# Column halves for the last output bank, and a third scratch pair for the first weight narrowings

## Chip, cores and metric

The kernel runs on one core of one Trainium2 chip. The metric is the device time of one execution in microseconds (us), as the median of several runs.

## What is computed

A Nyström attention, then a gated two-layer network, then a second two-layer network, all in float32 precision. Cut to what matters:

```python
# q, k, v: (4 batches, 8 heads, 576 tokens, 64); 32 landmarks are means of 18 tokens each
A  = softmax(q @ k_lm^T / 8);  Bm = softmax(q_lm @ k_lm^T / 8);  C = softmax(q_lm @ k^T / 8)
Z  = Bm^T / (norms);  six times: Z = 2 Z - Z @ Bm @ Z
x  = (A @ Z @ C @ v)                      # as 2304 tokens x 512
xn = x / rms(x) * rms_g
x  = (silu(xn @ w_gate) * (xn @ w_val)) @ w_out          # 512 -> 1536 -> 512
out = (s * relu(x @ w_in2)**2 + b) @ w_out2              # 512 -> 2048 -> 512
```

The five weight matrices arrive as float64 words and are narrowed to float32 on the chip.

## The kernel before, in words

**One list, planned ahead.** The kernel does not emit instructions as it goes. It first makes a list of operations (`op`), each with the engines that may run it, an estimated duration, a key (its due time) and the buffers that it reads and writes. Then `Scheduler.run` (line 174) walks through estimated time, and at each step gives an engine the ready operation with the smallest key. What it emits is a fixed order for each engine's queue and for SP's DMA queue; on the chip each engine runs its queue in that order and waits where data is not there. A `Ring` is a set of slots; a `Buf` takes a free slot of its ring when its first operation is emitted, and gives it back after its last. A queued ring hands out slots in the order in which its Bufs were made. `gate` (line 1485) is an operation of no cost that waits for a list of others and then frees slots that were marked as held.

**The first network's start.** Weights are handled in 12 column blocks `f` of 128. `first_weights` (line 1167) narrows block f of w_gate and of w_val into one of three slots of `rawg`, and stores the result to DRAM for later batches (`keptg`). `narrow` (line 1112) does one matrix block: SP loads 512 KB of float64 words into a staging slot; ScalarE (ACT) writes two scratch tiles, `ca_all` (line 1145) and `cmag_all` (lines 1147 and 1155; in place of 1155 VectorE, DVE, can run 1156); DVE combines the two into the destination (line 1159). The scratch tiles have two slots each (`ca_r`, `cm_r`, line 358), so two narrowings can be between their first ACT instruction and their DVE combination at a time. `fused` (line 1289) multiplies the narrowed block by the batch's value matrix on TensorE (PE) into two PSUM banks (line 1299), and ACT and DVE evacuate it as `u` (lines 1311, 1312, 1314). `hidden` (line 1337) then runs the products of u with the normalised attention rows (line 1326) and the gated activation (ACT line 1343, DVE lines 1345 and 1349). `fused` and `hidden` share four banks, `gv_r`, two of which batch 1's attention also uses. `out_weights` (line 1181) narrows blocks of w_out into two slots of `rawo` (`ro_r`, line 355); these are first written when block 0 of w_out is combined.

**The end.** The second network's output is accumulated token block by token block (`second_mm`, line 1407): 128 tokens by 512 columns fill one PSUM bank, three products (high and low parts) for each of 16 blocks f. The last token block, `j = NB - 1`, has 256 tokens, two banks (`c` = 0 and 1). After its last block f, each bank is copied to a staging tile by one ACT or DVE instruction (lines 1426 and 1427) and stored by four transfers of 32 rows, two from SP's queue and two from ACT's (line 1432). A transfer's 32 rows lie 18 output rows apart; the four groups of 32 are neighbours: row 18 i + n for i = 0 to 31, and n rises by one from one transfer to the next.

Of the kernel before, what the change touches and what calls it, by code (L numbers as in the profile page):

```python
# [38 lines left out]
N_SUM = 2  # L39
XB = 1  # L40
# [233 lines left out]
def t_dma(kb, n=1):  # L274
    return DMA_LAG + max(DMA_KB * kb, 0.45 * n)
# [10 lines left out]
def t_mm(n):  # L286
    return 0.0004167 * (max(n, 200) + 32)
# [7 lines left out]
def tile_nystrom_attention_two_mlps(  # L295
# [62 lines left out]
    ca_r, cm_r = (Ring([Slot(x[:, 512 * i:512 * i + 512]) for i in range(2)], True) for x in c_all)  # L358
# [753 lines left out]
    def narrow(key, kind, f, part, dst, w, after=()):  # L1112
# [3 lines left out]
        st, a, m = Buf(st0_r if rows else st_r), Buf(ca_r), Buf(cm_r)  # L1116
# [45 lines left out]
        if rows:  # L1162
            row_ops.extend(S_.ops[n_ops:])
        for o in S_.ops[n_ops + 1:]:
            o.after = RELC
# [240 lines left out]

    def second_mm(key, j, f, w, wn, hs, off):
# [5 lines left out]
        for c in range(nt):  # L1413
            def mm(_, c=c):
                s = slice(off + 128 * c, off + 128 * c + 128)
                for i, (a, y) in enumerate(PART3):
                    nc.tensor.matmul(out=A[c].t, lhsT=hs[a].t[:, s], rhs=w.t[:, 512 * y:512 * y + 512],  # L1417
                                     start=(f == 0 and i == 0), stop=(f == F2 - 1 and i == 2))

            op(("pe", 3 * t_mm(512)), key + 0.65 * c, mm, r=[*wn, *hs], w=[A[c]]).mode = "r"  # L1420
        if f < F2 - 1:
            return
        for c in range(nt):
# [12 lines left out]
            if j < NB - 1:  # L1436
                op(("sp", t_dma(256, 4)), key, lambda e, store=store: store(e, range(4)), r=[o])
                continue
            op(("sp", t_dma(128, 2)), key, lambda e, store=store: store(e, (0, 1)), r=[o])
            op(("act", 1.1), key, lambda e, store=store: store(e, (2, 3)), r=[o])  # L1440
# [83 lines left out]

    n_out = [0]
# [7 lines left out]
    for n in range(N_T):  # L1533
        t = T[n]
        todo = len(o_at.get(n, []))
        if n < len(units):
            b, f = units[n]
            if n == F1:
                gate("near", row_ops, t)
            if f == 0:  # L1540
                if b + 1 < B:
                    attention(b + 1, *at_time(b + 1))
                    S_.by_path(batch_ops[b + 1], *at_time(b + 1))
                else:
                    gate("attn", at_ops, t, free_w2)
            u = us.pop((b, f))
            hidden(t, t + 0.85, b, f, 0, u)
            t += 2 * t_first
# [234 lines left out]
```

## Time and profile before

| | |
|---|---|
| median of 3 runs | 829.31 us (828.41 to 831.85) |
| profiled execution, its own time | 829.26 us |
| its span (first to last instruction) | 827.5 us |
| PE busy | 810.5 us, 98% |
| weight loads of PE | 653.3 us, 79% |
| DVE busy | 651.0 us, 79% |
| ACT busy | 531.4 us, 64% |
| GpSimd (POOL) busy | 119.8 us, 14% |

How to read it: the busy shares are averages over stages with different limits. PE's busy time holds 43 matmuls on a constant that only keep it active before the first products, and matmuls that wait inside a group. So a stage has to be read by itself: which engine is full there, and what the first useful work waits for.

### The profile page before, as it was taken

To read this page: it belongs to the slowest core of one execution; us is meant where nothing else is said; L and a number is where in the kernel's file an instruction comes from. 1 tells how busy PE (TensorE), PEld (TensorE's weight loads), DVE (VectorE), ACT (ScalarE), POOL (GpSimd) and SP (SyncE) were. 2 spreads that over 40 slices of the span, in tenths; PEclk is the share of its full clock that TensorE was granted. 3 is DMA by queue.
4 is the path that set the end of the run, shared out by engine and by line. 5 is a ranking of instruction groups with operands and counts; after the bars stand their busy time and mean duration, and the time that the engine had idled before them with its cause. 6 is when DMAs were issued, how large, how long until landed. Compare 5 with 4: busy or idle time off the path is not lost.

```text
span 827.5 us, 16641 instructions
## 1 busy us (share of the span) xinstructions
PE 810.5 (98%) x6151; PEld 653.3 (79%) x6151; DVE 651.0 (79%) x1461; ACT 531.4 (64%) x1097; POOL 119.8 (14%) x173
## 2 busy tenths in 40 slices
PE   8899999999999999999999999999999999999997
PEld 5577767877787877888888888887888888888886
DVE  6888998777787777898998988799766767665554
ACT  5899987543534434688888976578555556565553
POOL 0370355117411132210100000000000000000000
PEclk9999999999999999999999999999999999999999
DMA  9999959652542313398978641232422432254234
GB/s 281 326 381 368 266 178 285 222 135 81 144 139 89 128 47 125 116 295 274 321 260 316 199 169 51 90 102 70 135 77 76 112 93 80 75 164 140 64 87 130
DMA packets 87234, 138.46 MB, mean 167 GB/s; under 512 B 26480, under 2 KB 49008, under 8 KB 87152
## 3 DMA queue, kind: packets, MB, share of 16 engines
q1 hardware_dynamic: 86960, 137.13, 52.3%
q8 instruction: 48, 0.79, 0.4%
q14 instruction: 34, 0.28, 0.1%
q10 hardware_dynamic: 192, 0.26, 0.1%
HBM read 114.82 MB, written 22.54 MB: 166 GB/s over the span
## 4 chain that ended last, share of the span: by engine, by line
PE 79%; DVE 11%; ACT 5%; DMA 2%; issue 2%; POOL 0%; DVEq 0%; SPq 0%; ACTq 0%; POOLq 0%
PE bank L1417 23%; PE bank L1282 17%; PE bank L1390 14%; PE bank L1326 14%; PE bank L1664 3%; PE bank L1299 3%; PE bank L754 1%; DVE w_all L1108 1%; DVE hl L1108 1%; DVE hbuf L1345 1%; PE bank L1372 1%; ACT ca_all L1145 1%; PE bank L675 1%; DMA stage<-in_moe_w_out_dram 1%; DVE rawg L1159 1%
## 5 line engine op out<-in xcount | busy, mean ns | idle before, releaser
L1417 PE MATMUL bank<-w_all,hh 128*128 128x512 f32 x472 | 148.0, 394 | 0.0
L1390 PE MATMUL bank<-hh,w_all 128*128 128x512 f32 (+1 forms) x448 | 144.6, 379 | 0.1
L1417 PEld LDWEIGHTS bank<-w_all,hh 128*128 128x128 f32 x472 | 88.2, 188 | 20.3
L1390 PEld LDWEIGHTS bank<-hh,w_all 128*128 128x128 f32 x448 | 81.6, 188 | 24.1 <-issue 9.5
L1417 PE MATMUL bank<-w_all,hl 128*128 128x512 f32 x236 | 93.1, 394 | 0.0
L1326 PE MATMUL bank<-xh,u_all 128*128 128x288 f32 x400 | 88.2, 300 | 0.5 <-DVE hbuf L1345 0.3
L1390 PE MATMUL bank<-hl,w_all 128*128 128x512 f32 (+1 forms) x224 | 83.0, 370 | 0.0
L1108 DVE TENSOR_TENSOR w_all<-rawo,w_all 128x512 fp32r<-128x512 f32 x86 | 62.1, 722 | 12.8 <-ACT w_all L1106 10.0
L1326 PEld LDWEIGHTS bank<-xh,u_all 128*128 128x128 f32 x400 | 66.2, 188 | 4.6 <-issue 1.0
L1343 ACT ACTIVATE hbuf<-bank 128x288 f32<-128x288 f32 x96 | 38.9, 405 | 32.4 <-PE bank L1326 30.2
L1326 PE MATMUL bank<-xl,u_all 128*128 128x288 f32 x200 | 59.0, 295 | 0.2 <-DVE xl L1090 0.2
L1326 PE MATMUL bank<-xh,xl 128*128 128x288 f32 x184 | 54.2, 295 | 0.0
L1326 PE MATMUL bank<-xl,xh 128*128 128x288 f32 x184 | 54.2, 294 | 0.0
L1417 PEld LDWEIGHTS bank<-w_all,hl 128*128 128x128 f32 x236 | 44.3, 188 | 10.6
L1345 DVE SCALAR_TENSOR_TENSOR hbuf<-hbuf,bank 128x288 f32<-128x288 f32 x96 | 42.5, 443 | 8.8 <-ACT hbuf L1343 8.3
L1106 ACT ACTIVATE w_all<-rawo 128x512 fp32r<-128x512 f32 x48 | 30.3, 631 | 28.7 <-PE bank L1390 14.6
L1390 PEld LDWEIGHTS bank<-hl,w_all 128*128 128x128 f32 x224 | 42.2, 188 | 5.5 <-DVE hl L1108 0.3
L1106 ACT ACTIVATE hh<-hbuf 128x288 fp32r<-128x288 f32 (+8 forms) x73 | 26.6, 389 | 21.9 <-PE bank L1390 13.9
L1585 ACT ACTIVATE xbuf<-xbuf,b_sb,s_sb 128x512 f32<-128x512 f32 (+1 forms) x34 | 26.0, 765 | 20.2 <-DVE xbuf L1596 19.7
L1155 ACT ACTIVATE cmag_all<-stage 128x512 f16<-128x512 f32 x48 | 37.9, 790 | 1.0
L1326 PEld LDWEIGHTS bank<-xl,u_all 128*128 128x128 f32 x200 | 37.6, 188 | 1.2 <-DVE xl L1090 0.4
L1108 DVE TENSOR_TENSOR hl<-hbuf,hh 128x512 fp32r<-128x512 f32 (+8 forms) x76 | 36.9, 495 | 1.6 <-ACT hh L1106 0.2
(316 smaller groups left out, 1940.3 us busy)
## 6 DMA issues: line engine op xcount, KB each, us to landing
rawg<-keptg SPq DMA_DIRECT2D x36, 512.0 KB, 4.4
stage<-in_moe_w_out_dram SPq DMA_DIRECT2D x28, 512.0 KB, 5.5
rawo<-kepto SPq DMA_DIRECT2D x48, 256.0 KB, 3.1
rawg<-kept SPq DMA_DIRECT2D x24, 512.0 KB, 3.6
rawo<-kept SPq DMA_DIRECT2D x36, 256.0 KB, 2.6
stage<-in_moe_w_in_dram SPq DMA_DIRECT2D x16, 512.0 KB, 5.4
keptg<-rawg SPq DMA_DIRECT2D x12, 512.0 KB, 6.1
kept<-tail SPq DMA_DIRECT2D x24, 256.0 KB, 3.7
```

Source lines behind the costliest of these rows:

```text
L1106: e.activation(out=hi(), in_=src(), func=ACTF.Copy) if e is nc.scalar
L1108: b = op({"dve": t_dve(n), "pool": t_pool(n)}, key, lambda e: e.tensor_tensor(out=lo(), in0=src(), in1=hi().bitcast(F32), op=ALU.subtract) ...
L1155: e.activation(out=upper(), in_=word(1).bitcast(F32), func=ACTF.Copy, scale=2.0 ** -100)
L1282: nc.tensor.matmul(out=ps.t, lhsT=a[h][:, 128 * kd:128 * kd + 128], rhs=x[kd][y].t, start=(first and kd == 0 and i == 0), stop=(last and k ...
L1299: nc.tensor.matmul(out=pU[g].t[m, 256 * j:256 * j + 256], lhsT=gw[b].t[p, m], rhs=r.t[p, :, 128 * k:128 * k + 128], start=True, stop=True)
L1326: nc.tensor.matmul(out=ps.t[:, 0:HC], lhsT=u[a].t[:, 256 * g + 128 * part:256 * g + 128 * part + 128], rhs=x[y].t.rearrange("p k n -> p (k ...
L1343: op(("act", t_act(HC)), tg, lambda e: e.activation(out=th.t[:, 0:HC], in_=pg.t[:, 0:HC], func=ACTF.Tanh, scale=0.5), r=[pg], w=[th])
L1345: op(("dve", t_dve(HC)), tg, lambda e: e.scalar_tensor_tensor(out=th.t[:, 0:HC], in0=th.t[:, 0:HC], scalar=1.0, in1=pg.t[:, 0:HC], op0=ALU ...
L1390: nc.tensor.matmul(out=A[c].t[:, 0:n], lhsT=w[a].t[:, 128 * c:128 * c + 128], rhs=hs[y].t[:, 0:n], start=(f == 0 and i == 0), stop=(f == F ...
L1417: nc.tensor.matmul(out=A[c].t, lhsT=hs[a].t[:, s], rhs=w.t[:, 512 * y:512 * y + 512], start=(f == 0 and i == 0), stop=(f == F2 - 1 and i = ...
L1585: e.activation(out=h.t[:, c:c + n], in_=h.t[:, c:c + n], func=ACTF.Identity, scale=s_sb, bias=b_sb) if e is nc.scalar
L1664: nc.tensor.matmul(out=ps.t[:, 0:n], lhsT=tot.t[:, 1024 * a + c:1024 * a + c + 128], rhs=xs[3, kd // 2][y].t[:, n * (kd % 2):n * (kd % 2) ...
```

## The change

There are two edits, which do not touch each other.

**The last bank.** In the last block f of the last token block, the products of the last bank (c = 1) are issued for columns 0 to 255 and then for columns 256 to 511: six matmuls of 256 columns in place of three of 512. A new function, `last_out`, copies both banks of the last token block in two halves of 256 columns: for each half ACT or DVE, but for the last half of the last bank DVE alone. Bank c = 0 is stored by one transfer from SP of 128 rows by 512 columns; bank c = 1 by one transfer from ACT for the first half and one from SP for the second, each of 128 rows by 256 columns. The transfer's destination is indexed (n, i, column) with n = 0 to 3 and i = 0 to 31; its source is 128 partitions by columns.

**The third scratch slot.** The narrowings of w_gate and w_val for f = 0, 1, 2 (`C_F = 3`, six narrowings) take their scratch from rings with a third slot: `rawo`'s slot 0 as `ca`, `rawo`'s slot 1 as `cmag`. Both slots of `rawo` are held until a gate has seen all six through, and then serve w_out as before. The six have queues of their own (`ca0_r`, `cm0_r`) on the shared slots.

```diff
+C_F = 3
-    ca_r, cm_r = (Ring([Slot(x[:, 512 * i:512 * i + 512]) for i in range(2)], True) for x in c_all)
+    c_two = [[Slot(x[:, 512 * i:512 * i + 512]) for i in range(2)] for x in c_all]
+    ca_r, cm_r = (Ring(x, True) for x in c_two)
+    c_more = [Slot(ro_r.slots[0].t), Slot(ro_r.slots[1].t.bitcast(I32))]
+    ca0_r, cm0_r = (Ring(x + [y], True) for x, y in zip(c_two, c_more))
+    c_ops = []
+    for x in ro_r.slots:
+        x.held = True
...
-        st, a, m = Buf(st0_r if rows else st_r), Buf(ca_r), Buf(cm_r)
+        early = rows and f < C_F
+        st, a, m = Buf(st0_r if rows else st_r), Buf(ca0_r if early else ca_r), Buf(cm0_r if early else cm_r)
...
+        if early:
+            c_ops.extend(S_.ops[n_ops + 1:])
...
+    def last_out(key, j, A):
+        c0, n = blocks[j]
+        nt = n // 128
+        for c in range(nt):
+            o = Buf(os_r)
+            for d in range(2):
...
+                e = {"act": t_act(256), "dve": t_dve(256)} if c < nt - 1 or d == 0 else {"dve": t_dve(256)}
+                op(e, key, copy_out, r=[A[c] if c < nt - 1 else (A[c], d), "stage"], w=[(o, d)])
+
+            def store(e, x, m, ds, c=c, o=o):
+                bb, n_ = divmod((c0 + 128 * c) // 32 + x, SEG)
+                cols = slice(256 * ds[0], 256 * ds[-1] + 256)
+                e.dma_start(
+                    out=out[bb * S:bb * S + S, :].rearrange("(i n) d -> n i d", n=SEG)[n_:n_ + m, :, cols],
+                    in_=o.t[32 * x:32 * x + 32 * m, cols])
+
+            if c < nt - 1:
+                op(("sp", t_dma(256, 1)), key, lambda e, store=store: store(e, 0, 4, (0, 1)), r=[(o, 0), (o, 1)])
+                continue
+            op(("act", 0.5), key, lambda e, store=store: store(e, 0, 4, (0,)), r=[(o, 0)])
+            op(("sp", t_dma(128, 1)), key, lambda e, store=store: store(e, 0, 4, (1,)), r=[(o, 1)])
...
+            halves = 2 if j == NB - 1 and f == F2 - 1 and c == nt - 1 else 1
+            for d in range(halves):
+                def mm(_, c=c, d=d, m=512 // halves):
...
+                        nc.tensor.matmul(out=A[c].t[:, m * d:m * d + m], lhsT=hs[a].t[:, s],
+                                         rhs=w.t[:, 512 * y + m * d:512 * y + m * d + m],
...
+        if j == NB - 1:
+            last_out(key, j, A)
...
-            op(("sp", t_dma(128, 2)), key, lambda e, store=store: store(e, (0, 1)), r=[o])
-            op(("act", 1.1), key, lambda e, store=store: store(e, (2, 3)), r=[o])
...
+    def free_c(_):
+        for x in ro_r.slots:
+            x.held, x.free = False, 0.0
...
+            if n == 2:
+                gate("c", c_ops, -1.0, free_c)
```

## Rows read from the trace of the kernel before

**Rows 1.** Windows: stretch, length, busy of PE, PEld, DVE, ACT, POOL (instructions), clock, DMA

```profile
0.00:39.20 39.20, 34.12 (x472) 20.22 (x473) 30.34 (x113) 26.66 (x66) 6.29 (x14) 1.00 1.03 309
39.20:49.70 10.50, 8.38 (x77) 5.87 (x75) 9.24 (x18) 10.27 (x21) 9.20 (x12) 1.00 1.04 335
49.70:80.00 30.30, 30.30 (x299) 25.04 (x294) 26.40 (x68) 29.30 (x59) 6.28 (x10) 1.00 1.04 376
80.00:120.00 40.00, 37.84 (x475) 27.89 (x476) 37.45 (x92) 35.34 (x79) 16.28 (x22) 1.00 0.86 251
823.40:827.50 4.10, 0.00 (x0) 0.00 (x0) 0.63 (x1) 0.00 (x0) 0.00 (x0) 0.90 0.46 128
```

**Rows 2.** Timeline of PE, 37 to 50 us: start, duration, engine, line, operation

```profile
37.91 1.68 PE L1746 MATMUL bank<-ones 128*128 128x512 bf16 x7
39.24 0.48 PE L1326 MATMUL bank<-xh,u_all 128*128 128x288 f32 x1
...
39.69 0.42 PE L1326 MATMUL bank<-xh,u_all 128*128 128x288 f32 x2
39.95 0.30 PE L1326 MATMUL bank<-xl,u_all 128*128 128x288 f32 x1
...
46.33 1.22 PE L1299 MATMUL bank<-rawg,gw 64*32 64x256 f32 x16 [0.88 <-DVE hbuf L1345]
...
48.75 0.99 PE L1299 MATMUL bank<-rawg,gw 64*32 64x256 f32 x16 [0.40 <-DVE u_all L1314]
49.67 0.40 PE L1326 MATMUL bank<-xh,u_all 128*128 128x288 f32 x1
```

**Rows 3.** Timeline of ACT, 26 to 35 us

```profile
26.07 0.67 ACT L1145 ACTIVATE ca_all<-stage 128x512 f32<-128x512 f32 x1
...
27.32 0.78 ACT L1155 ACTIVATE cmag_all<-stage 128x512 f16<-128x512 f32 x1
30.64 2.53 ACT L1043 ACTIVATE region<-bank 128x288 f32<-128x288 f32 x8 [2.54 <-PE bank L1037]
...
33.25 0.75 ACT L1145 ACTIVATE ca_all<-stage 128x512 f32<-128x512 f32 x1
```

**Rows 4.** Timeline of DVE, 30 to 46 us

```profile
31.99 0.76 DVE L1048 TENSOR_TENSOR region<-region 128x576 f32<-128x576 f32 x1 [0.85 <-ACT region L1043]
...
36.24 0.66 DVE L1159 SCALAR_TENSOR_TENSOR rawg<-ca_all,cmag_all 128x512 int32<-128x512 int32 x1
...
40.36 0.68 DVE L1159 SCALAR_TENSOR_TENSOR rawg<-ca_all,cmag_all 128x512 int32<-128x512 int32 x1
...
43.15 2.76 DVE L1159 SCALAR_TENSOR_TENSOR rawg<-ca_all,cmag_all 128x512 int32<-128x512 int32 x2
```

**Rows 5.** Timeline of all engines, the last 6 us; SPq and ACTq are DMA issues

```profile
822.46 0.62 PE L1417 MATMUL bank<-region,hh 128*128 128x512 f32 x2
822.65 0.60 ACT L1426 ACTIVATE stage<-bank 128x512 f32<-128x512 f32 x1 [4.31 <-PE bank L1417]
...
822.91 0.39 PE L1417 MATMUL bank<-region,hl 128*128 128x512 f32 x1
823.28 1.75 SPq L1432 DMA_DIRECT2D out_dram<-stage  x4
823.28 1.83 ACTq L1432 DMA_DIRECT2D out_dram<-stage  x4
823.33 0.69 DVE L1427 COPY stage<-bank 128x512 f32<-128x512 f32 x1 [3.12 <-PE bank L1417]
```

**Rows 6.** DMA, 823 to 827 us: queue, packets, MB, share of 16 engines

```profile
q1 hardware_dynamic: 192, 0.26, 29.7%
q10 hardware_dynamic: 192, 0.26, 17.7%
```

**Rows 7.** DMA, 46.8 to 48.6 us, when rows of 1 KB were loaded

```profile
q1 hardware_dynamic: 655, 0.65, 109.7%
```

**Rows 8.** DVE timeline: a copy of 256 columns out of a PSUM bank

```profile
47.82 0.42 DVE L1312 CAST u_all<-bank 128x256 fp32r<-128x256 f32 x1
```

More of the change, by code (lines that the diff above doesn't have):

```diff
@@ L1405, in tile_nystrom_attention_two_mlps, with copy_out @@
     acc = {}
+    def last_out(key, j, A):
[4 more added lines that the diff above has]
+            for d in range(2):
+                def copy_out(e, c=c, d=d, o=o):
+                    x, y = o.t[:, 256 * d:256 * d + 256], A[c].t[:, 256 * d:256 * d + 256]
+                    if e is nc.scalar:
+                        e.activation(out=x, in_=y, func=ACTF.Copy)
+                    else:
+                        e.tensor_copy(out=x, in_=y)
+                e = {"act": t_act(256), "dve": t_dve(256)} if c < nt - 1 or d == 0 else {"dve": t_dve(256)}
[11 more added lines that the diff above has]
+            op(("sp", t_dma(128, 1)), key, lambda e, store=store: store(e, 0, 4, (1,)), r=[(o, 1)])
     def second_mm(key, j, f, w, wn, hs, off):
@@ L1413, in second_mm @@
         for c in range(nt):
[L1414 to L1420, printed above, removed]
+            halves = 2 if j == NB - 1 and f == F2 - 1 and c == nt - 1 else 1
+            for d in range(halves):
+                def mm(_, c=c, d=d, m=512 // halves):
+                    s = slice(off + 128 * c, off + 128 * c + 128)
+                    for i, (a, y) in enumerate(PART3):
+                        nc.tensor.matmul(out=A[c].t[:, m * d:m * d + m], lhsT=hs[a].t[:, s],
+                                         rhs=w.t[:, 512 * y + m * d:512 * y + m * d + m],
+                                         start=(f == 0 and i == 0), stop=(f == F2 - 1 and i == 2), skip_group_check=j == NB - 1 and c == nt - 1)
+                op(("pe", 3 * t_mm(512 // halves)), key + 0.65 * c + 0.3 * d, mm, r=[*wn, *hs],
+                   w=[A[c]] if halves == 1 else [(A[c], d)] + ([] if d else [A[c]])).mode = "r"
         if f < F2 - 1:
+            return
+        if j == NB - 1:
+            last_out(key, j, A)
             return
@@ L1434, in store @@
                         in_=o.t[32 * i:32 * i + 32, :])
-            if j < NB - 1:
-                op(("sp", t_dma(256, 4)), key, lambda e, store=store: store(e, range(4)), r=[o])
-                continue
-            op(("sp", t_dma(128, 2)), key, lambda e, store=store: store(e, (0, 1)), r=[o])
-            op(("act", 1.1), key, lambda e, store=store: store(e, (2, 3)), r=[o])
+            op(("sp", t_dma(256, 4)), key, lambda e, store=store: store(e, range(4)), r=[o])
     LEAD, LEAD_O = 6, 5
```

## The prediction

> **What bounds the kernel now.** I read the busy time of each engine by stage first [rows 1], then the timelines of the two places that the change touches. From 49.7 to 80 us PE has no idle time at all (30.30 of 30.30 us) and ACT nearly none (29.30); the same holds, less strictly, to 120 us (37.84 and 35.34 of 40). Before that the picture differs. From 39.2 to 49.7 us ACT is full (10.27 of 10.50) and DVE nearly so (9.24), while PE idles 2.1 us. What busy PE time there is before 39.2 us is partly filler: the seven matmuls on a constant at 37.91 us end where the first hidden product starts, at 39.24 us [rows 2]. That product belongs to column block f = 0; the products of f = 1 start only at 49.67 us, behind two groups of line 1299 that took 1.22 and 0.99 us and waited for DVE [rows 2]. So the start-up is a relay in which ACT narrows weights, DVE combines them, and PE runs as they come. At the other end nothing computes for the last 4.1 us of the span but one copy [rows 1]: it is copy, issue, traffic, landing and closing.
>
> **The third scratch slot.** It removes a wait. The second narrowing leaves ACT at 28.1 us (27.32 + 0.78); the third starts only at 33.25 us, although ACT idles 2.54 us before the squares of line 1043 at 30.64 us [rows 3]: both scratch slots are taken until DVE has combined the first. With a third slot the third narrowing can run in that gap. Its three ACT instructions are two of 0.67 and one of 0.78 us, 2.1 us together [rows 3], and fit into 2.54. Its combination, 0.66 us, fits into DVE's idle 0.85 us before 31.99 us [rows 4]. From then on each narrowing of a full ACT comes one place earlier. The combination at 36.24 us then finishes f = 1, which before was finished by the one at 40.36 us [rows 4]: four us sooner, and in time for line 1299 of f = 1 to replace filler before 39.24 us. Then DVE's pair at 43.15 us (2.76 us for two, where one alone takes 0.68) becomes a single combination.
>
> The worth: f = 1 is ready 4 us sooner, but PE had only 2.1 us of idle time to give back there, and the full ACT behind it hands on just the 2.1 us of one narrowing. Both give 2.1, so I take **-2.1 us**. Bounds: -4.3, if PE's idle time of 80 to 120 us (2.2 us more) goes too; +2.1, if the planner puts the trio in front of an instruction that the attention chain waits for. No instruction is added. What is moved past the queues: SP issues the loads that wait for staging slots as much earlier as ACT frees them, the store of f = 1 too. DMA is full (share 1.04 [rows 1]), but a load that only follows its slot moves with it. The held slots of rawo are wanted only when w_out's first block is combined, after the six; a gate on the six costs nothing while that order holds, else DVE would stand until it opens.
>
> **The last bank.** Four steps.
> (a) PE: six products of 256 columns for three of 512. Two of 512 start 0.45 us before the next (822.46 to 822.91), so 0.68 for three [rows 5]; at 288 columns two start 0.26 us before the next [rows 2], so six take at most 0.78: +0.1 us at most.
> (b) Copy: the last half costs 0.42 [rows 8] for 0.69 [rows 5]: -0.27, if the first half is copied while the second is multiplied. No row shows PE writing and another engine reading one bank at once; if they take turns, two copies of 0.42 follow the last product, and the step is +0.15.
> The Trainium skill, "PSUM — Partial Sum Buffer", section "PSUM bank collisions raise a hardware error", says that two engines may not be in one bank and quadrant at once, other columns included, and that software must keep them apart; by that the step is +0.15, and the sum 0.4 us higher. No run here shows it.
> (c) Issue: four transfers from each queue took 1.75 us on SP, 0.44 each [rows 5]. The last bank has one for each queue in place of two: -0.44. ACT's store of the first half queues behind ACT's own copies; nothing follows it.
> (d) Traffic: 512 KB either way. Before, eight transfers of 32 rows make 256 packets of 2 KB. The queues' shares of 16 engines over 4 us are 19.0 and 11.3 engine-us [rows 6]: 30.3 in all, 1.9 us on 16 engines. Each queue's 192 packets are 128 rows and 64 small ones, 16 for each transfer: every transfer of 32 rows was dealt to 16 engines, two rows each. The new transfers have an outermost count of 4 (n), and n and i cannot be merged, since their strides are one row and 18. How such a shape is dealt no row shows. If over its rows, all 16 engines carry it; if along its outermost count, four do. At four, each carries 32 packets of 2 KB (bank 0) and 64 of 1 KB (bank 1). Prices: 88 ns for 2 KB (11.3 / 128, the queue that was not held up [rows 6]) and 48 ns for 1 KB (1.097 x 16 x 1.8 us / 655 [rows 7]). That is 2.8 + 3.1 = 5.9 us for 1.9: +4.0. The traffic can start 0.2 us sooner, with bank 0's copy of 0.42 for 0.60. Under four engines (b) and (c) are hidden behind the traffic of bank 0, so the end costs **+3.8 us**. Under 16 it is traffic-bound too, and (b) to (d) give about -0.3 (from -0.7, all of copy and issue, to +0.4). I take four, because a dealing along the outermost count also explains two of 32 rows per engine with no rule about strides.
> The Trainium skill, "DMA: Bandwidth & Descriptors", section "Why a DMA increments its semaphore by 16 and not by 1", says that the engines used are the largest number up to 16 that divides the slowest dimension of both sides, here 4 and 128. By that it is four. No run here shows it yet.
> Upper bound for four: at the mean price of both queues (30.3 / 256 = 118 ns, and 1 KB in proportion) 7.9 us, +6.0; at the price of the slower queue (19.0 / 128 = 148 ns) 9.9 us, +8.0.
>
> **Sum.** The profiled execution took 829.26 us, its span 827.5; the median of the runs is 829.31, so one stands for the other. 829.3 - 2.1 + 3.8 = **831.0 us**.
>
> **The rivals.**
> A. The transfers run on 16 engines. Then the end gives 0.3 back: 829.3 - 2.1 - 0.3 = 826.9. For it: all transfers of the trace here looked at are on 16. Against it: none has an outermost count below 16.
> B, slower. The packets of the two queues hold each other up on the four engines, as they did on 16, where one queue's packets cost 148 ns and the other's 88 [rows 6]. Place: the three last stores. Price: +8.0, so 829.3 - 2.1 + 8.0 = 835.2. It decides the sign once the end costs over 6.2 us, at 1.4 times the prices that I took. Against it: four engines ask less of the memory than 16.
> C. The slot's gain does not reach PE. Line 1299 of f = 1 waited for DVE [rows 2], which freed banks there, and DVE is 88% busy; if banks and DVE set that time, the early narrowing only waits longer. 829.3 + 3.8 = 833.1.
>
> **How the numbers follow.** Forecast 0.52, A 0.20, B 0.14, C 0.14. About what a measurement can tell from no change is 0.5%, 4.1 us: 825.2 to 833.5. Faster needs A with the slot's bound of -4.3: 0.06. Slower is B and the upper part of C: 0.19. Within: 0.75. The range reaches from the lower half of A, 826.0, to just short of B, 834.4; what is left out is about 0.07 below and 0.1 above. The likeliest case alone, with its own bounds for slot and copy, spans 829 to 833.
>
> **What would show it.** Slot: the third narrowing's ACT trio at 28 to 30.5 us, line 1299 of f = 1 before 40, and its first product well before 49.67; PE's idle time of 39 to 50 us gone. End: the number of small packets for each last store (4 is four engines, 16 is all), and the time from the last product to the span's end, now 4.2 us: 8 under four engines, under 4 under 16. Wrong would be a plan that differs widely behind 50 us, so that the middle gives or takes more than an us: then neither sum holds.

## The result, and the profile after

The changed kernel takes 838.78 us as the median of five executions (834.78 to 840.04), against 829.31 for the kernel before in the same comparison; the ratio is 1.0088, with a 95% interval of 1.0069 to 1.0107. That is 7.3 us by the ratio and 9.5 by the medians: slower, and outside the range of 826.0 to 834.4. The executions of one kernel differ by some us, and the longer ones are mostly those with the lower mean granted clock (after: 0.996 and 0.997 in the two below 836, 0.989 to 0.993 in the three above 838), so below medians and intervals are compared, and the clock is part of the account.

The profiled execution took 839.89 us, its span is 838.1 where before it was 827.5. Of the 10.6 us more, the trace shows two places. At the end, the last product ends at 828.14 and the span 10.0 us later, where before it was 823.30 and 4.2: +5.8 us. The rest, 4.8 us, has come about by the last product. The windows of the changed kernel (columns as in [rows 1]):

```profile
0.00:39.20 39.20, 34.17 (x465) 20.33 (x466) 29.61 (x111) 28.40 (x68) 6.27 (x14) 0.96 1.00 312
39.20:49.70 10.50, 8.13 (x47) 6.15 (x46) 9.04 (x16) 6.57 (x13) 7.75 (x12) 0.68 1.03 297
49.70:80.00 30.30, 29.27 (x268) 24.11 (x266) 24.21 (x60) 28.29 (x60) 6.66 (x10) 1.00 0.93 321
...
828.00:838.10 10.10, 0.14 (x2) 0.00 (x0) 0.42 (x1) 0.50 (x2) 0.00 (x0) 0.65 0.18 52
```

Against [rows 1], ACT is no longer full from 39.2 to 49.7 us (6.57 of 10.50 us, 10.27 before), but PE has done less there, 47 matmuls for 77, and the granted clock was 0.68 where it had been 1.00: the 1.2 GHz level for most of the stretch. The last row has a DMA share of 0.18.

The slot itself did what the change says. ACT's timeline around 28 us (answers [rows 3]; line 1153 was 1145, line 1163 was 1155):

```profile
27.60 0.78 ACT L1163 ACTIVATE cmag_all<-stage 128x512 f16<-128x512 f32 x1
28.25 0.65 ACT L1153 ACTIVATE rawo<-stage 128x512 f32<-128x512 f32 x1
...
29.49 0.78 ACT L1163 ACTIVATE rawo<-stage 128x512 f16<-128x512 f32 x1
30.91 2.53 ACT L1050 ACTIVATE region<-bank 128x288 f32<-128x288 f32 x8 [0.64 <-PE bank L1044]
```

The third narrowing runs from 28.25 to 30.27 us in the gap that ACT had before. But PE's timeline (answers [rows 2]; line 1309 was 1299, line 1336 was 1326) begins later, not earlier:

```profile
40.29 1.11 PE L1309 MATMUL bank<-rawg,gw 64*32 64x256 f32 x16
41.32 0.61 PE L1336 MATMUL bank<-xh,u_all 128*128 128x288 f32 x1
...
43.41 0.29 PE L1336 MATMUL bank<-xh,u_all 128*128 128x288 f32 x1
46.07 0.61 PE L1336 MATMUL bank<-xh,u_all 128*128 128x288 f32 x1 [2.37 <-DVE hbuf L1355]
...
48.88 0.65 PE L1336 MATMUL bank<-xh,u_all 128*128 128x288 f32 x2
```

Line 1309 of f = 1 now comes ahead of the first hidden product, which starts at 41.32 us (39.24 before). After twelve matmuls, the first half of f = 0, PE waits for DVE's line 1355 until 46.07; before, PE had no such wait until 46.33 us, and then one of 0.88 [rows 2]. The second half has twelve more, so the second matmul of the pair at 48.88 us is the first product of f = 1: it starts at 49.1 us, where before it started at 49.67. DVE's and POOL's timelines say what DVE was doing (line 1167 was 1159, line 1355 was 1345; answers [rows 4]):

```profile
42.14 1.69 DVE L1097 TENSOR_TENSOR xl<-tail,xh 128x288 fp32r<-128x288 f32 x1
43.76 1.90 DVE L1167 SCALAR_TENSOR_TENSOR rawg<-ca_all,cmag_all 128x512 int32<-128x512 int32 x1
45.57 0.44 DVE L1355 SCALAR_TENSOR_TENSOR hbuf<-hbuf,bank 128x288 f32<-128x288 f32 x1
```

```profile
42.09 3.01 POOL L587 TENSOR_TENSOR region<-region 128x576 f32<-128x576 f32 x2
```

A subtraction that takes 0.45 us elsewhere took 1.69, and a combination that takes 0.68 took 1.90, both while two POOL instructions of 1.5 us each ran. The combination belongs to the fifth narrowing (f = 2), and it is queued in front of line 1355.

The end, all engines, and the DMA from 828 to 838 us (answers [rows 5, 6]; 10 us of 16 engines are 160 engine-us):

```profile
827.46 1.09 ACT L1426 ACTIVATE stage<-bank 128x256 f32<-128x256 f32 x3 [4.25 <-PE bank L1458]
...
827.86 0.28 PE L1458 MATMUL bank<-region,hl 128*128 128x256 f32 x1
828.15 1.45 SPq L1436 DMA_DIRECT2D out_dram<-stage  x2
828.59 1.16 ACTq L1436 DMA_DIRECT2D out_dram<-stage  x1
828.59 0.42 DVE L1428 COPY stage<-bank 128x256 f32<-128x256 f32 x1 [3.92 <-ACT stage L1426]
```

```profile
DMA packets 396, 0.52 MB, mean 52 GB/s; under 512 B 12, under 2 KB 268, under 8 KB 396
...
q1 hardware_dynamic: 264, 0.39, 14.8%
q10 hardware_dynamic: 132, 0.13, 3.7%
```

Three transfers left 12 small packets, four each, where before each left 16. The packets took 23.7 and 5.9 engine-us, 29.6 in all; on four engines that is 7.4 us, on 16 it would be 1.9. Three of the four half copies ran on ACT one behind the other, and DVE's, the fourth, began only when ACT had ended. ACT was at bank 0's two halves until 828.2 us, so its copy of the last bank's first half did not start before the last product had ended (828.14).

### The profile page after: what moved, and what is told of

It reads as the page before. It is cut to its first block, busy times and chain, and to the rows that moved or that the text cites. A ratio compares the mean times of both kernels' runs of the same rounds, so it can differ in the third digit from the quotient of the medians.

```text
span 838.1 us, 16636 instructions
## 1 busy us (share of the span) xinstructions
PE 813.9 (97%) x6148; PEld 656.0 (78%) x6148; DVE 651.2 (78%) x1458; ACT 535.0 (64%) x1102; POOL 118.9 (14%) x175
## 4 chain that ended last, share of the span: by engine, by line
PE 81%; DVE 9%; ACT 6%; DMA 2%; issue 1%; POOL 0%; SPq 0%; DVEq 0%; ACTq 0%; POOLq 0%
PE bank L1458 23%; PE bank L1292 16%; PE bank L1336 15%; PE bank L1400 14%; PE bank L1712 3%; PE bank L1309 3%; PE bank L1382 2%; PE bank L761 1%; DVE w_all L1115 1%; PE bank L682 1%; DMA region<-in_q_dram 1%; DMA region<-in_k_dram 1%; PE bank L1085 1%; ACT ca_all L1153 1%; DVE hl L1115 1%
## 5 line engine op out<-in xcount | busy, mean ns | idle before, releaser
L1113 ACT ACTIVATE w_all<-rawo 128x512 fp32r<-128x512 f32 x53 | 33.5, 632 | 32.8 <-PE bank L1400 14.6
L1458 PEld LDWEIGHTS bank<-w_all,hl 128*128 128x128 f32 x236 | 44.4, 188 | 10.6
```

The source lines that it names most:

```text
L1113: e.activation(out=hi(), in_=src(), func=ACTF.Copy) if e is nc.scalar
L1458: nc.tensor.matmul(out=A[c].t[:, m * d:m * d + m], lhsT=hs[a].t[:, s], rhs=w.t[:, 512 * y + m * d:512 * y + m * d + m], start=(f == 0 and ...
```

## Theories and experiments

Theory of the end: the four engines are the cost, not the copies in halves. Theories of the start: C, the slot is worth nothing, and what is lost is lost through the granted clock; S, the slot's order costs the time whatever the clock does; P, it is lost where DVE meets POOL. Each run below was set against the kernel before on the same chip; n is the number of executions.

**The two halves of the change, each alone, and the kernel before again.** The end alone:

```diff
-C_F = 3
+C_F = 0
...
-    for x in ro_r.slots:
-        x.held = True
...
-            if n == 2:
-                gate("c", c_ops, -1.0, free_c)
```

> The change without the third scratch slot: scratch rings of two slots as before, rawo never held; the last bank as in the change. Theory E (the end costs what its own trace shows, 10.0 us from the last product to the span's end in place of 4.2, and the rest of the changed kernel's loss belongs to the start-up): 829.3 + 5.8 = 835.1 us, and the last product ends where it does before, at about 823.2 us. Theory P (my forecast's price of the end): 829.3 + 3.8 = 833.1. Rival M (the split last bank also changes the plan of the middle): the last product ends more than 1 us later than 823.2, and the time is 836.5 or more.

835.35 us (n = 5, 834.82 to 836.33), ratio 1.0061 (1.0049 to 1.0074). The last product ended at 823.35 us, 10.05 before the span's end. So the end costs 5.8 us by the trace and 5.1 to 5.3 by the times, and leaves the middle alone. These executions have mean clocks of 0.995 to 0.997, although in the trace the clock is 1.00 from 20 to 60 us: the mean takes in the 10 us at the end, where it is 0.68. The two executions of the whole change with 0.996 and 0.997 (834.8 and 835.7 us) lie where the end alone lies.

The slot alone, with the end of the kernel before (`last_out` and the six half products taken out; cut, against the changed kernel):

```diff
-        if j == NB - 1:
-            last_out(key, j, A)
-            return
...
+            op(("sp", t_dma(128, 2)), key, lambda e, store=store: store(e, (0, 1)), r=[o])
+            op(("act", 1.1), key, lambda e, store=store: store(e, (2, 3)), r=[o])
```

> The third scratch slot alone; the last bank as before. My forecast: 829.3 - 2.1 = 827.2 us. Theory C (the granted clock of 0.50 between 35 and 50 us in the changed kernel's trace is not the slot's doing but falls in some executions of either kernel; without it the slot is worth nothing): 829.3 to 829.9, single executions at 832 to 834, and in those the mean clock is lower than in the others. Rival S (the slot itself brings the lower clock or delays the start): 832 to 834 in every execution, with a first product of f = 0 at 41 us in place of 39.2.

833.50 us (n = 12, 829.28 to 835.56), ratio 1.0030 (1.0014 to 1.0046). Three executions lay at 829.3 to 830.0 with a mean clock of 0.999 or 1.0, nine at 832.5 to 835.6 with 0.993 to 0.996. The two ratios add up to 1.0091, the whole change had 1.0088: there are two separate costs. My gain of 2.1 us showed in none of the twelve.

The kernel before, unchanged:

> The kernel before once more, for the granted clock of each of its executions. Theory C: its times fall in two groups, 828.4 to 829.4 with a mean clock of 0.998 or more and 831.7 to 832 with a clock of about 0.995, the difference of 2.5 to 3 us being what a lower clock in the start-up costs. Rival S: the clock of all its executions is 0.998 or more, and the scatter has nothing to do with it.

830.15 us (n = 12, 828.89 to 832.37): seven at 828.9 to 830.2 with 0.998 or more, five at 831.2 to 832.4 with 0.995 to 0.998. So the kernel before has such executions too, 1 to 2 us longer; theory C had said 2.5 to 3, and one of the five, 832.0, had a mean of 0.998, so the mean clock orders them only roughly. On another chip two of its 17 executions took 834.1 and 834.3 us, with 0.993. The profiled one, which with 830.18 us is one of the seven, shows a fall in a window (columns as in [rows 1]):

```profile
20.00:36.00 16.00, 13.71 (x284) 8.42 (x283) 13.88 (x47) 13.31 (x33) 5.82 (x9) 1.00 1.07 376
36.00:42.00 6.00, 5.96 (x24) 3.26 (x24) 5.68 (x15) 5.38 (x12) 0.96 (x2) 0.72 1.01 198
42.00:46.00 4.00, 3.75 (x30) 3.44 (x30) 3.13 (x4) 3.80 (x9) 4.00 (x4) 1.00 1.00 324
```

In the trace of before the same first window had PE busy 13.69 us and the second a clock of 1.00: the same kernel, the same work, and the clock falls at 37 us in one execution and not in the other. With this one fall, and PE busy right behind it (3.75 of 4 us), the execution took 0.9 us more than the profiled one of before (829.26).

**The stores alone.** The kernel before, its last two banks copied whole, with

```diff
-            op(("sp", t_dma(128, 2)), key, lambda e, store=store: store(e, (0, 1)), r=[o])
-            op(("act", 1.1), key, lambda e, store=store: store(e, (2, 3)), r=[o])
+            def store_4(e, c=c, o=o):
+                bb, n_ = divmod((c0 + 128 * c) // 32, SEG)
+                e.dma_start(out=out[bb * S:bb * S + S, :].rearrange("(i n) d -> n i d", n=SEG)[n_:n_ + 4], in_=o.t)
+            op(("sp", t_dma(256, 1)) if c < nt - 1 else ("act", 0.5), key, lambda e, store_4=store_4: store_4(e), r=[o])
```

> The kernel before with the stores of the last two banks alone changed: each bank is copied whole as before, then stored by one transfer of 128 rows by 512 columns with the destination indexed (n, i, column), bank 0 from SP, bank 1 from ACT. Theory F (four engines per transfer make the end long): 4 small packets per transfer; 64 packets of 2 KB per engine at 90 ns (twice the 45 ns of a 1 KB packet on ACT's queue in the changed kernel) to 140 ns (its SP queue) are 5.8 to 9.0 us in place of 1.9, so the end is 8 to 11 us and the time 833.2 to 836.4. Rival K (the copies in halves, one after the other, make the end long): the time stays within 829.3 +- 0.8 and the end at 4 to 5 us.

835.56 us (n = 6; five at 834.46 to 835.67, the profiled one at 841.46), ratio 1.0072 (1.0049 to 1.0095). In the profile the last product ended at 830.02 and the span at 839.7: 9.7 us, though no copy is split. DMA from 829 to 839 us:

```profile
DMA packets 264, 0.52 MB, mean 52 GB/s; under 512 B 8, under 2 KB 8, under 8 KB 264
...
q1 hardware_dynamic: 132, 0.26, 10.5%
q10 hardware_dynamic: 132, 0.26, 6.7%
```

Four small packets for each transfer, 27.5 engine-us, 6.9 us on four engines: theory F, and K falls. The last product ended 6.7 us later than before. That comes neither from the stores, which stand behind it, nor from the slot, which this kernel hasn't: the clock was 0.50 from 36 to 42 us, PE waited 1.93 us at 52 us for DVE's line 1314, queued behind a combination that took 1.97 us while POOL's line 580 ran, and the clock fell again (0.50 from 54 to 56 us).

**Half copies on 16 engines.** The end alone again, with the tokens of the last block in the order (i, n), so that a transfer's outermost count is 32:

```diff
+            def by(x, p):
+                return x.t[:, 0:m].rearrange(p, i=32, n=4) if j == NB - 1 else x.t[:, 0:m]
+            to, fro = "p (g i n) -> p g n i", "p (g n i) -> p g n i"
-            split(key - 4, lambda: hh.t[:, 0:m], lambda: hl.t[:, 0:m], lambda: h.t[:, 0:m],
+            split(key - 4, lambda: by(hh, to), lambda: by(hl, to), lambda: by(h, fro),
-                    out=out[bb * S:bb * S + S, :].rearrange("(i n) d -> n i d", n=SEG)[n_:n_ + m, :, cols],
-                    in_=o.t[32 * x:32 * x + 32 * m, cols])
+                    out=out[bb * S:bb * S + S, :].rearrange("(i n) d -> i n d", n=SEG)[:, n_:n_ + m, cols],
+                    in_=o.t[:, cols])
```

> The changed end without the third slot, with the rows of the last token block dealt differently: the high and low parts of the last block's hidden values are written with the tokens in the order (i, n) instead of (n, i), so that partition 4 i + n of a bank holds output row 18 i + n, and each of the three transfers has an outermost count of 32 in place of 4. Products, copies in halves, queues and bytes are those of the changed end. Theory F (the dealing to four engines makes the end long): 16 small packets per transfer, an end of about 4.2 us (copies one after the other 0.9, an issue 0.7, 128 KB of traffic about 0.8, 1.8 from there to the span's end, as in the kernel before), so 829.3 us where the clock stays at 1.00. Rival K (single transfers or half copies are slow in themselves): the end stays at 8 to 10 us and the time at 833 to 835.

830.38 us (n = 12), ratio 1.0003 (0.9994 to 1.0012): all 5 us of the end are back. Timeline and DMA (824 to 829 us) of its end; the span ends at 828.4, 4.2 us behind the last product:

```profile
823.51 1.09 ACT L1424 ACTIVATE stage<-bank 128x256 f32<-128x256 f32 x3 [4.23 <-PE bank L1456]
...
823.90 0.28 PE L1456 MATMUL bank<-region,hl 128*128 128x256 f32 x1
...
824.63 0.67 ACTq L1434 DMA_DIRECT2D out_dram<-stage  x1
```

```profile
DMA packets 432, 0.52 MB, mean 105 GB/s; under 512 B 48, under 2 KB 304, under 8 KB 432
...
q1 hardware_dynamic: 288, 0.39, 22.0%
q10 hardware_dynamic: 144, 0.13, 7.7%
```

48 small packets for three transfers, 16 each, and 23.8 engine-us, 1.5 us on 16. The copies are in halves and one behind the other as in the change, and the end is as long as before. What the change lost at its end is the dealing to four engines alone.

The kernel with the stores alone changed, in the same order of rows (with the lines `by`, `to` and `split` as above):

```diff
-                e.dma_start(out=out[bb * S:bb * S + S, :].rearrange("(i n) d -> n i d", n=SEG)[n_:n_ + 4], in_=o.t)
+                e.dma_start(out=out[bb * S:bb * S + S, :].rearrange("(i n) d -> i n d", n=SEG)[:, n_:n_ + 4], in_=o.t)
```

> The kernel before with the last block's hidden values written in the order (i, n), each of the last two banks copied whole as before and stored by one transfer of outermost count 32 (bank 0 from SP, bank 1 from ACT). Theory F: 16 small packets per transfer; one issue of 0.7 us in place of four that take 1.75 in a row, so the last 64 KB start about 1 us sooner, and the traffic is 1.9 us on 16 engines: the end takes 3.5 to 4.2 us in place of 4.2, and the time is 828.6 to 830.2 in place of the 830.2 that the kernel before has as its median over all executions on this chip.

830.50 us (n = 12), ratio 0.9995 (0.9981 to 1.0010), the end 4.1 us; theory F had 828.6 to 830.2. Single transfers on 16 engines are no measurable gain over four transfers of 32 rows.

**More and less filler.** To see what the clock does with the slot, the filler matmuls that the planner puts between 20 and 36 us were doubled (10 more) or left out (10 fewer), in the kernel before and in the kernel with the slot alone:

```diff
                     warm(t)
+                    if 20.0 < t < 36.0:
+                        warm(t)
```

and

```diff
-                    warm(t)
+                    if not 20.0 < t < 36.0:
+                        warm(t)
```

> The third slot alone, as before, and every filler matmul that the planner puts between 20 and 36 us doubled: 10 more matmuls on the constant (about 2 us of PE time in the places where it idles), so that PE is busier ahead of the point where the granted clock fell. Theory C (the clock's fall costs the time, the slot is worth nothing): if the clock stays at 1.00, all executions at 829.3 to 830, as those three of the twelve with the slot alone that had a mean clock of 0.999 or 1.0. My forecast: 827.2 with a held clock. Rival S (the slot's order itself costs the 3 us, the clock falls as a consequence): 832 to 834 even with a clock of 1.00 up to 42 us. If the clock falls as before, nothing is told.

> The kernel before with the same doubled filler between 20 and 36 us. Theory C: if the clock then stays at 1.00, its times come in one group at 829 to 829.8 in place of two (829 to 830.3 and 830.7 to 832.4). If the added filler holds the chain up, up to 2 us more in all executions.

> The kernel before without the 10 filler matmuls that the planner puts between 20 and 36 us (the counterpart of the runs with 10 more). Theory C (PE idling ahead of 36 us lets the granted clock fall, and that is worth 2 to 3 us to the kernel before): the clock falls in every execution, times 831 to 832.5, in one group. Rival N (the filler has no part in it): times as before, 829 to 832.4 with most below 830.3.

> The third slot alone, without the same 10 filler matmuls. Theory C with P (the slot's order is more exposed to the fall: the delay puts DVE's early combination and the activation behind POOL's sums, PE idles 3.5 us and the clock falls a second time): all executions at 832.5 to 836, so 2 to 4 us above the kernel before without filler, where with doubled filler the two were equal (830.74 and 830.90). Rival S (the slot costs or gains the same whatever the clock does): the difference to the kernel before without filler is that with doubled filler, 0 within 0.5 us.

Medians, with the mean granted clocks of the executions:

| | 10 fewer | as planned | 10 more |
|---|---|---|---|
| before | 833.72 (n = 6; 0.990 to 0.992) | 830.15 (n = 12; 0.995 to 1.0) | 830.90 (n = 12; 0.998 to 1.0) |
| slot alone | 836.70 (n = 6; 0.988 to 0.991) | 833.50 (n = 12; 0.993 to 1.0) | 830.74 (n = 11; 0.997 to 1.0) |
| difference | +3.0 | +3.3 | -0.2 |

The columns were measured on different chips, with medians of the kernel before as it was of 830.65, 830.03 and 830.37 us beside them; the ratios to these are 1.0037, 1.0003 and 1.0007 for before and 1.0075, 1.0030 and 1.0004 for the slot. With 10 more the slot and the kernel before are the same (0.9995 to 1.0012 and 0.9997 to 1.0016), and the 827.2 of my forecast for a held clock did not come. With the filler as planned or fewer the slot costs about 3 us. Without the slot, 10 fewer cost 3.1 us by the ratio (833.72, above the 832.5 that was expected at most); the slot with 10 fewer was above its 836 too, but 3.0 above the kernel before with 10 fewer, as theory C had it and rival S had not. And the scatter of the kernel before did not go with 10 more (829.68 to 832.35, clock 0.998 or more), so not all of it is the clock's; that expectation failed. Windows of the slot with 10 more, of the slot alone and of before with 10 fewer, in this order:

```profile
36.00:42.00 6.00, 5.74 (x50) 3.83 (x48) 4.90 (x14) 5.84 (x14) 0.43 (x2) 1.00 1.06 242
```

```profile
36.00:42.00 6.00, 5.96 (x36) 3.42 (x36) 4.48 (x13) 4.85 (x12) 0.38 (x2) 0.72 1.06 235
42.00:46.00 4.00, 0.50 (x4) 0.27 (x3) 4.00 (x5) 2.63 (x5) 4.00 (x4) 1.00 1.02 294
46.00:50.00 4.00, 4.00 (x20) 4.00 (x20) 3.44 (x7) 1.82 (x4) 4.00 (x8) 0.57 1.04 358
...
130.00:135.00 5.00, 4.76 (x28) 2.78 (x28) 4.10 (x14) 4.92 (x8) 1.84 (x3) 0.67 0.94 244
```

```profile
20.00:36.00 16.00, 12.54 (x261) 8.27 (x261) 12.29 (x43) 11.70 (x29) 5.81 (x9) 0.79 1.07 375
36.00:42.00 6.00, 4.99 (x22) 3.43 (x22) 4.36 (x13) 5.00 (x11) 0.00 (x0) 0.64 0.85 192
```

With the slot alone the clock falls at 36 to 42 us, once more at 46 to 50, after PE has idled 3.5 us, and a third time at 130 to 135 us; this last fall the slot with 10 more has too (0.76 in that window). After the same 0.72 from 36 to 42 us the kernel before had PE busy for 3.75 us of the next 4, the slot for 0.50 us. That idle time, in the timelines of PE and of DVE, slot alone:

```profile
45.73 0.41 PE L1336 MATMUL bank<-xh,u_all 128*128 128x288 f32 x1 [3.50 <-DVE hbuf L1355]
```

```profile
41.81 1.68 DVE L1097 TENSOR_TENSOR xl<-tail,xh 128x288 fp32r<-128x288 f32 x1
43.41 1.90 DVE L1167 SCALAR_TENSOR_TENSOR rawg<-ca_all,cmag_all 128x512 int32<-128x512 int32 x1
```

and the same place with 10 more, PE, DVE and POOL (there the lines are 1338, 1357, 1099, 1169 and POOL's 589):

```profile
43.23 0.40 PE L1338 MATMUL bank<-xh,u_all 128*128 128x288 f32 x1 [1.05 <-DVE hbuf L1357]
```

```profile
41.76 0.45 DVE L1099 TENSOR_TENSOR xl<-tail,xh 128x288 fp32r<-128x288 f32 x1
42.13 0.68 DVE L1169 SCALAR_TENSOR_TENSOR rawg<-ca_all,cmag_all 128x512 int32<-128x512 int32 x1
```

```profile
41.71 3.79 POOL L589 TENSOR_TENSOR region<-region 128x576 f32<-128x576 f32 x2
```

Both DVE instructions ran undisturbed here, and POOL's pair took 3.79 us instead of 3.00: this time POOL waited. The slot without filler shows the other outcome again, 1.68 and 1.90 us and a wait of 3.48. In the other traces of the slot with this order the two go together: DVE waited where the clock had fallen before (the whole change, 10 fewer), POOL where it had held (the two whole changes with 10 more below, 3.79 us in both). In the kernel before, the pair of combinations that meets POOL (2.76 us for two [rows 4]) stands behind the activation of the first block; what waits for it is the next activation, and with that PE for 0.88 us at 46.33 [rows 2]. I had read that row as a price for a pair and had not asked why it was so high.

**Order and meeting point.** If the meeting with POOL is the whole loss, moving the combination or POOL's start should cure it, with the filler as planned:

```diff
-                narrow(key + 2.6 * part, 1, f, part, lambda part=part: r.t[:, part], (r, part))
+                narrow(key + 2.6 * part, 1, f, part, lambda part=part: r.t[:, part], (r, part),
+                       [hid[0, 0, 0]] if (f, part) == (2, 0) else ())
```

```diff
-                        out=mark, in_=part(1)[:, cols][:, 0:1].bitcast(F32)), r=wl, w=["sums"])
+                        out=mark, in_=part(1)[:, cols][:, 0:1].bitcast(F32)), r=[*wl, (pair[1], ("a", hf, 0))], w=["sums"])
```

> The third slot alone, with one order on DVE changed: the combination of the fifth narrowing (w_gate, f = 2) may run only when batch 0's first hidden block is done, so DVE's activation pair (lines 1356 and 1360) comes ahead of it; with the slot alone it stood in front of that pair, took 1.90 us in place of 0.68 while POOL's sums ran, and PE idled 3.50 us. Theory P (a DVE instruction on SBUF operands waits for a whole POOL instruction; which of the two comes first at 41.8 us decides, and the early combination is queued in front of what PE waits for): the subtraction at 41.8 us can still be held up by 1.2 us, the combination no longer matters; PE's idle time there is at most 2.3 us, and no execution is above 832; median 829.5 to 831. Theory C (only the granted clock ahead of 42 us decides; the filler is as with the slot alone): two groups as before, most executions at 832.5 to 835.5.

With the first edit alone 832.73 us (n = 10), ratio 1.0033 (1.0017 to 1.0049), as with the slot alone: theory P's forecast fell. The subtraction still took 1.68 us; the wait in its place was down to 0.53 us, but the clock was 0.72 from 36 to 42 us all the same, and fell again at about 100 us (0.70 from 98 to 102 us, with 1.1 us of PE waiting for DVE's line 937).

> As the run before, and the POOL instruction that starts POOL's sums for batch 1 also waits for the last of the four subtractions of batch 0's first normalisation, so neither that subtraction nor the fifth combination can meet POOL's sums ahead of the activation. Theory P: PE's idle time between the two halves of f = 0 is at most 1.1 us, as in the run with doubled filler, and all executions lie at 828.5 to 830.5, whatever the clock does up to 42 us. Theory C: most executions at 832.5 to 835.5.

With both 831.03 us (n = 11, 829.94 to 832.76), ratio 1.0011 (1.0001 to 1.0021). The four subtractions and the activation were undisturbed, and the combinations behind them met POOL:

```profile
39.11 1.56 DVE L1097 TENSOR_TENSOR xl<-tail,xh 128x288 fp32r<-128x288 f32 x4
40.60 0.76 DVE L1325 TENSOR_TENSOR u_all<-bank,u_all 128x256 fp32r<-128x256 f32 x2
41.73 0.46 DVE L1356 SCALAR_TENSOR_TENSOR hbuf<-hbuf,bank 128x288 f32<-128x288 f32 x1 [0.38 <-ACT hbuf L1354]
...
42.66 1.58 DVE L1167 SCALAR_TENSOR_TENSOR rawg<-ca_all,cmag_all 128x512 int32<-128x512 int32 x1
```

Some 0.9 of the 2.5 us is left. Nothing lay above 832.8. Four of the eleven were still at 832.2 to 832.8 with a clock of 0.996 to 0.998, above theory P's 830.5; but the kernel before reached 832.1 in this comparison, so that bound was too tight for either kernel. In the profiled execution the clock was 1.00 from 20 to 60 us, so it doesn't part the stall from the fall. With the first edit the long wait was gone and the loss was not; with the kernel before again there was a fall and hardly a loss. So neither P nor the clock alone is the account. What parts the traces is how often the clock falls: with at most one stretch at 0.50 ahead of the last product the executions took 829.3 to 831.5 us (with the end on four engines 835.1 and 836.1), with two or more 832.8 to 836.3 (839.9 and 841.5). In each of these six one of the falls came right behind a wait of PE for DVE, of 1.0 to 3.5 us; but waits of 1.05 us (10 more) and 1.3 us (both edits) passed without a fall. That the wait brings the fall is argued, not shown.

**Both causes out of the whole change** (the doubled filler and the order (i, n), edited as above), then the doubled filler alone:

> The whole change with both causes taken out: the last block's hidden values are written in the order (i, n), so that its three transfers have an outermost count of 32, and the filler between 20 and 36 us is doubled. If the dealing to four engines and the granted clock of the start-up are all that the change lost, it is back at the time of the kernel before with doubled filler, 830.3 to 831.2 us. If another cost stands in the whole change that neither half shows alone, it stays at 832 or more.

830.61 us (n = 11), ratio 1.0004 (0.9995 to 1.0013).

> The whole change with the filler between 20 and 36 us doubled, the end as the change has it. If the causes add up: the 830.7 of the slot with doubled filler plus 5.0 to 5.8 for the end, 835.7 to 836.5 us, in place of 838.8. If the slot's loss in the whole change isn't the clock's, it stays at 838 to 840.

836.14 us (n = 5), ratio 1.0067 (1.0053 to 1.0081). Within these intervals, 0.1% either way, the two causes add up and are all that the change lost. The second is taken out here by the filler, and with that the clock and the meeting change together. No version measured here beats the kernel before.

## The prediction, step by step

**The third scratch slot, -2.1 us: wrong by sign.** Everything up to PE came as written: the trio at 28.25 to 30.27 us, each narrowing one place earlier. Line 1309 of f = 1 came at 40.29 instead of before 40 and did replace filler (37 matmuls on the constant in place of 43); the first product of f = 1 came at 49.1, half a us sooner, instead of well before 49.67. The step that failed is "PE had only 2.1 us of idle time to give back there", as time that an earlier f = 1 gives back. Where the clock held, f = 1 came 6 us sooner, and PE gave back nothing. With 10 more filler, the slot (the first product of f = 1 is the second matmul of the first row, at 44.9 us) and then the kernel before:

```profile
44.80 0.42 PE L1338 MATMUL bank<-xh,u_all 128*128 128x288 f32 x2
...
50.52 0.55 PE L622 MATMUL bank<-ident,region 128*128 128x128 f32 x3 [0.97 <-DVE xl L1326]
...
325.73 0.64 PE L1065 MATMUL bank<-ones,region 128*96 128x1 f32 x6 [0.40 <-DVE hbuf L1357]
```

```profile
50.86 0.41 PE L1328 MATMUL bank<-xh,u_all 128*128 128x288 f32 x1
```

New waits take the place of the idle time. Line 1309 of f = 1 fills two banks ahead of the hidden products, and the second half of f = 0 then waits for DVE's line 1355, which reads a bank of the first half: 1.05 us with 10 more filler, 2.37, 3.50 and 3.48 in the whole change, the slot alone and the slot with 10 fewer. Then the transposes of batch 1's attention (line 622 here, 620 in the slot alone) wait for DVE to empty a bank of f = 2: 0.97 us, and 0.99 in the slot alone. These two, 1.05 and 0.97, come to 2.0 of the 2.1 us. The plan behind 50 us differs a little too: between 325 and 331 us PE waits some 0.4 us for DVE in all eight traces with the slot, and in none of the eight without it. From 36 to 60 us PE is busy 21.71 of 24 us with the slot and 21.73 without (both with 10 more filler, clock 1.00). That is rival C's mechanism, "banks and DVE set that time". C priced the slot at 0, which is what it is worth where the clock holds (-0.2, with some 0.7 us of doubt in each median); with the filler as planned it costs 2.5 us by the ratio (1.2 to 3.8), about my bound of +2.1. The bound's place, an instruction "that the attention chain waits for", was near: it is DVE's combination, not ACT's trio, that stands in front of one. I never listed what a combination that is moved forward on DVE is moved past, or which engine it meets there. The Trainium skill, "SBUF — State Buffer", section "SBUF: two separate sides", says that DVE, with two SBUF operands, and GpSimd take an exclusive lock on a shared pair of ports for a whole instruction. The traces agree: 0.45 became 1.69 and 0.68 became 1.90 next to POOL's 1.5 us, while line 1355, one of whose operands is in PSUM, kept its 0.44. POOL's recorded start stands 0.05 us ahead of DVE's both where DVE waited and where POOL did, so the records do not tell which of them has the ports first.

**The granted clock: not in the prediction at all.** I took the 43 filler matmuls as something that could be replaced by earlier products, and the clock of 1.00 in one execution [rows 1] as given. It is not given: it falls in some executions of either kernel, and with the filler as planned or fewer the slot's order takes about 3 us more. No term of the sum held a wait that is followed by a second fall.

**The end, +3.8 us: right in mechanism, too small.** Four engines, as I took it, by four small packets for each transfer. The Trainium skill, "DMA: Bandwidth & Descriptors", section "Why a DMA increments its semaphore by 16 and not by 1", has a rule that gives 4 engines for an outermost count of 4 and 16 for one of 32. The runs agree: 4 and 16 small packets. Rival A, 16 engines, fell. The term that was mis-sized is the traffic: 5.9 us forecast, 7.4 measured. The 1 KB packets on ACT's queue cost 46 ns each (5.9 us / 128; I had 48), but those on SP's queue took 23.7 us; with 128 of 1 KB at 46 ns in it, an estimate, its 2 KB packets come to 139 ns, not 88. I had priced bank 0, which SP stores, at the 88 ns of ACT's queue, although SP's own queue stood at 148 in [rows 6]. With the stores alone on four engines SP's 2 KB packets took 131 ns and ACT's 84; as single transfers on 16 engines they took 88 and 86. So rival B had the right price for half of the packets; its +8.0 charged it to all. Another 0.5 us came from the rest, of which the issue may be a part (1.16 us for ACT's transfer, 0.46 each before). From the last product to the end it is 10.0 us in place of the 8 that I wrote down, 1.5 of these 2.0 from the traffic.

**Copy and issue, (a) to (c):** PE's six half products start 0.12 us apart, inside the 0.13 that I had as the most, and two copies followed the last product, as in the case of "if they take turns"; but ACT came late because it was at bank 0's copies, so no run shows whether a half can be copied while the other is multiplied. What makes DVE wait for ACT's copy, the bank or the staging tile, the trace does not tell. The 0.4 us by which the prediction lets its sum rise if the two take turns would not have moved it: under four engines it hides (b) behind the traffic. On 16 engines the three steps together give nothing: 4.2 us as before, where rival A had -0.3.

**The sum and the range.** The two errors have the same sign: the end by 2.0 us and the slot by 4.6 (from -2.1 to +2.5) make 831.0 into 837.6, 1.2 below the measured median. The range was set by cases of which each took one thing going wrong; none had both.

**What stays open.** Why the fall comes more often with the slot (nine of its twelve executions above 832, none of eleven with 10 more filler, while PE's work from 20 to 36 us is the same, 13.63 us and 13.69 before) was not found, nor which executions without a profile had the stall. The double fall is not the slot's alone: the profile of the stores alone has it too. The wait for a bank was not taken away by itself.

## What to carry to other kernels

When an instruction is moved forward on a full engine, write down what it now stands in front of and which other engine is active at that time; a row that is several times longer than its kind (2.76 us for two that take 0.68) is a meeting to be named, not a price. Merging transfers is worth nothing if the merged shape is dealt to fewer engines: look at the small packets per transfer, and put a count that 16 divides outermost (32 here, for 4). Before filler is replaced by work that comes earlier, see in several executions whether the granted clock holds, and test a start-up with filler added and taken away.

## What the hardware showed that was not expected

- Ten filler matmuls more or fewer, some 2 us of PE time each way, go with 2 to 6 us of an 830 us kernel with the slot (ratios 1.0004, 1.0030, 1.0075), and ten fewer with 3 us without it (1.0003, 1.0037); in the traces of the slower ones the granted clock is down to 0.50 in stretches of the start-up. In the kernel before, the clock held in one trace and fell in another after the same PE work (13.69 and 13.71 us busy from 20 to 36 us).
- DVE and POOL meet in either order: two POOL sums took 3.00 us and DVE's two instructions 3.58 (slot alone), or DVE's took 1.13 and POOL's 3.79 (10 more), with POOL's start 0.05 us ahead of DVE's in both traces.
- The same transfer of 128 KB took ACT 1.16 us to issue when it was dealt to four engines, and 0.67 when dealt to 16. SP's transfer of 256 KB, which was issued first, took 0.68 and 0.62 (stores alone, in either order of rows); whether it is the engine or the second place that makes the difference no run tells.
